# Two layers of long convolution and MLP, forward and backward: moving the next chunk's gates on VectorE and six PSUM copies between VectorE and ScalarE

## The chip, the cores and the metric

The kernel runs on one core of a Trainium2 chip. Its engines are TensorE (PE; PEld is its weight load), VectorE (DVE), ScalarE (ACT), GpSimd (POOL) and SyncE (SP), and 16 DMA engines. The metric is the device time of one execution in microseconds, the median of several runs. Before the change it is 688.22 us (three runs, 687.91 to 688.73).

## The reference

The forward pass has two layers, each a gated long convolution (`A`) and an MLP (`B`), and the same weights serve both. The kernel returns the output and the gradients for eight inputs.

```python
def _A_ref(q, k, v, shift_k, ssm_k, ssm_D):      # S = 2048, D = 448
    kv = (k shifted by 0..3 rows, weighted by shift_k, summed) * v
    y = irfft(rfft(kv padded) * rfft(ssm_k padded))[:S] + kv * ssm_D
    return q * y
def _B_ref(x, w1, w2):                            # F = 1792
    return silu(x @ w1) @ w2
x = A_q
x = x + _A_ref(_layernorm(x), A_k, A_v, A_shift_k, A_ssm_k, A_ssm_D)
x = x + _B_ref(_layernorm(x), B_w1, B_w2)
x = x + _A_ref(_layernorm(x), A_k, A_v, A_shift_k, A_ssm_k, A_ssm_D)
x = x + _B_ref(_layernorm(x), B_w1, B_w2)
# outputs: x, and the gradients of A_q, A_k, A_v, A_shift_k, A_ssm_k, A_ssm_D, w1, w2 for grad_out
```

`k` and `v` do not change between the layers, so the convolution's result `y` is computed once. What a layer's `A` does to `x` is then a normalisation, a multiplication by `y` and an addition: the gate.

## The kernel before

The kernel has three parts. A prefix computes the convolution (up to about 84 us in the profile) and leaves its result in `Ysb`. `Main.run` then goes over the 2048 rows in four chunks of 512 (four tiles of 128 rows), from about 84 to 500 us. A suffix does the weight gradients and the gradients of the convolution.

For each chunk `Main` runs layer 1 (L = 0) and layer 2 (L = 1) forward and then both backward, and it weaves the backward of chunk c with the forward of chunk c + 1. The steps are Python generators, and each step emits one piece:

- `H`: the first product (w1) in 14 blocks of 128 columns, taken in pairs `fp` = 0 to 6. ScalarE writes Silu of a pair to `aT` (L833, or L816 in chunk 0) and a raw copy to `Dall` (L116). `slope` later turns `Dall` into the derivative of Silu in place (L843, six ScalarE instructions and a table load). In chunk 0 `Hh` does the same in half chunks, and VectorE takes some of the raw copies (L117).
- `O`: the second product (w2), one tile of 128 rows at a time, in two halves of seven matmuls (L850). VectorE adds the result to `X` (L855, "the output sum"). The last one traced is kept as `last_o`.
- `G`: the output gradient times w2 transposed, in pairs again (L681 full matmuls, L685 those with 64 rows of contraction). The copy out of PSUM goes to VectorE for the pairs named in `dv`, else to ScalarE. In layer 2 a later multiplication by the slopes stands at L1013. "Block" below means such a pair.
- `N`: the product with w1 transposed (L889) and the backward of the normalisations (`_ln_bwd`, L1063 to L1068, L905 to L917).
- `T` and `transp_half`: TensorE turns rows (L658, L669), and a copy brings them from PSUM to `nT`.
- `fwd0(c)`: layer 1's first half for a chunk. `_ln_parts` takes the statistics of a tile set (L309 to L313), raises the variance to the power -1/2 on POOL (L314) and normalises (L317). `gate` multiplies by `Y` and adds to `X` (L727, L728, two tiles at a time). Then a second `_ln_parts` normalises the new `X` to `n01`. Those rows are what `T` turns for the next `H`.
- `x_load(c)`: two SP DMAs (L739) that bring the chunk's rows of `A_q` to `xq`, a piece behind w1 and w2 in their tiles. They wait until the gates before have read it.

PSUM is shared by tags: `mm` (two buffers of two banks: `H`, `G`), `po` (two of one bank: `O`, `N`), `tr` (two: turned rows, and block 3 of `G`). In `G` the blocks are taken in groups of 2, 3 and 2. The first block of a group is followed at once by the 64-row matmuls of the others, so the banks of the whole group must be free there.

TensorE's instructions keep the order in which the program emits them. On the other engines and their DMA queues a planner orders the instructions: it simulates the kernel, and among those that its simulation takes to be ready it picks the earliest emitted, with two kinds of help. `tc.high_priority()` moves instructions ahead. `tc.issue_after(ins)` puts whatever the block emits on the engine of `ins` behind `ins` in that engine's queue. An engine then works through its queue strictly in order.

The loop over c in `run` begins with the slopes of layer 2, then `fwd0(c + 1)` queued behind `last_b` (the end of the first tile of `N` of layer 1; at c = 0 behind `last_dv`, a copy of `Hh`). Then it weaves `O` of layer 2 (the letter O), `G` of layer 2 (G), the remaining steps of `fwd0` (L, the generator `self.norm`) and `T`. At c = 0 two tiles of `O` and all of `G` have been emitted before the loop, so there is a short weave:

```python
if c == 0:
    weave("OOTOO", O=o, T=self.T(self.n0[1][1], nT, GBLK, engs=(nc.vector, nc.vector)))
```

Each tile of `O` takes two letters. At c = 0 the last output sum emitted before the weave is that of tile 1.

Of the kernel before, what the change touches and what calls it, by code (L numbers as in the profile page):

```python
# [212 lines left out]
def _hd(k, shape, name):  # L213
    return k.hd.tile(shape, BF16, name=name, tag="hd", bufs=3)
# [81 lines left out]
def _ln(k, pool, c, src, si, n_g, groups=((0, 4),), pin=False):  # L296
    for last in _ln_parts(k, pool, c, src, si, n_g, groups, pin):
        pass
    return last
# [39 lines left out]
def _ln_store(k, c, si, n_g):  # L339
    k.nc.gpsimd.dma_start(out=_pm(k.N_d[si][:])[:, 4 * c:4 * c + 4, :], in_=n_g[:])  # L340
# [272 lines left out]
GBLK = [(0, 128), (128, 256), (256, 384), (320, 448)]  # L613


class Main:
# [98 lines left out]
    def parts(fp):  # L715
        return [(0, 2)] if fp != 3 else [(0, 1), (1, 2)]

    def a_fwd(self, c, si, src, n_g, groups):
        _ln(self.k, self.ch, c, src, si, n_g, groups)
        self.gate(c, src, n_g)  # L720

    def gate(self, c, src, n_g, pairs=((0, 2), (2, 4)), pin=lambda i: i):
        nc, X = self.nc, self.X
        for lo, hi in pairs:
# [16 lines left out]
    def fwd0(self, c):  # L741
        k, nc = self.k, self.nc
        n01 = self.t([P, 4, D], "n01", bufs=2)
        if c == 0:
            xc, n00 = k.x0c0, k.na0
            self.first_norm(xc, n00, n01)
        else:
            n00 = _hd(k, [P, 4, D], "n00")
            xc = lambda tl: k.xq[tl.start // 2] if isinstance(tl, slice) else k.xq[tl // 2][:, tl % 2, :]
            self.a_fwd(c, 0, xc, n00, ((0, 4),))  # L750
            self.n0[c] = (n00, n01)
            norm = _ln_parts(k, self.ch, c, self.xs(c), 1, n01, ((0, 4),))
            next(norm)
            self.norm = self.fwd0_end(c, norm, n01)
            return
        _ln_store(k, c, 1, n01)
        self.n0[c] = (n00, n01)
# [8 lines left out]
            next(step)  # L766
        next(steps[1], None)

    def fwd0_end(self, c, norm, n01):
        with self.tc.issue_after(self.last_o.ins):  # L770
            next(norm, None)
        _ln_store(self.k, c, 1, n01)
        yield

# [154 lines left out]
    def run(self, ys):  # L929
        k, nc, tc = self.k, self.nc, self.tc  # L930
        self.n0, self.gyt = {}, {}
        jobs = k.jobs = Jobs(k, self)
        jg = jobs.gen()

        def weave(pattern, **gens):
            for ch in pattern:
                next(gens[ch], None)
            for g in gens.values():
                if g is not jg:
                    for _ in g:  # L940
                        pass

        gT, gh2 = self.nT(), []
        g = self.G(gT, gh2, groups=(1,) * 7)
        tg = self.T(k.gb0, gT, GBLK, engs=(nc.vector, nc.vector))
        nT = self.nT()
        go = lambda *gens: [next(x, None) for x in gens]
        go(tg, tg, ys, ys)
        with tc.high_priority():
            self.fwd0(0)  # L950
        go(ys, ys, ys, ys, ys, ys, g)
        with tc.high_priority():
            self.transp_half(self.n0[0][1], nT, GBLK, 0, nc.vector)
        go(g)
        self.Dall = k.mdp.tile([P, 2, 2, NF // 2, 512], BF16, name="Dall", tag="DA")
        self.w1T = k.wtp.tile([P, NF, D], BF16, name="w1T", tag="WT")
        with tc.issue_after(nc.sync.dma_start_transpose(out=self.w1T[:], in_=k.B_w1).ins):
            self.x_load(1)
        aT, dT1 = self.halves("aT", "T", 5), self.dT(0, 0)
        hs = [self.Hh(0, 0, nT, aT, dT1, 0, (1, 3), (1,)), self.Hh(0, 0, nT, aT, dT1, 1)]  # L960
        os_ = [self.O(0, 0, aT, (0, 1)), self.O(0, 0, aT, (2, 3))]
        go(hs[0], hs[0])
        with tc.high_priority():
            self.transp_half(self.n0[0][1], nT, GBLK, 1)
        go(hs[0], hs[0])
        go(*(hs[1], os_[0]) * 4)
        self.slope(dT1)
        with tc.high_priority():
            self.fwd1(0, ((0, 2),))
        with tc.issue_after(self.last_n.ins):  # L970
            go(*(os_[1],) * 4)
        go(g, g)
        with tc.high_priority():
            self.fwd1(0, ((2, 4),))
        nT = self.nT()
        aT, dT2 = self.halves("aT", "T", 5), self.dT(0, 1)
        hs = [self.Hh(0, 1, nT, aT, dT2, 0, (1, 3), (1,)), self.Hh(0, 1, nT, aT, dT2, 1)]
        r = [aT, dT2]
        with tc.issue_after(self.transp_half(self.n1[1], nT, GBLK, 0).ins):
            nc.scalar.activation(k.warm[:], k.mhalf[:], ACT.Silu)  # L980
        go(g, hs[0], hs[0], hs[0])
        self.transp_half(self.n1[1], nT, GBLK, 1)
        go(hs[0], g)
        o = self.O(0, 1, aT)
        go(*(hs[1], o) * 4, g)
        for c in range(4):

            aT2, dT2 = r
            self.slope(dT2)
            if c < 3:  # L990
                with tc.issue_after((self.last_b if c else self.last_dv).ins):
                    self.fwd0(c + 1)
                if c == 0:
                    next(self.norm)
            if c < 2:
                self.x_load(c + 2)
            nT = self.nT() if c < 3 else None
            if c > 0:
                o = self.O(c, 1, aT2)
            if c == 0:  # L1000
                weave("OOTOO", O=o, T=self.T(self.n0[1][1], nT, GBLK, engs=(nc.vector, nc.vector)))
            else:
                gh2 = []
                g = self.G(gT, gh2, dv=(1, 4))
                if c < 3:
                    weave("OOLOOGOGOGOGGOGTG", O=o, G=g, L=self.norm, T=self.T(self.n0[c + 1][1], nT, GBLK))
                else:
                    self.put()
                    jobs.start()
                    weave("GOOOOOOOOGGGGGG", O=o, G=g)  # L1010
            for hh in range(2):
                for lo, hi in ((0, 4), (4, 7)):
                    nc.vector.tensor_tensor(out=gh2[hh][:, lo:hi, :], in0=dT2[hh][:, lo:hi, :], in1=gh2[hh][:, lo:hi, :], op=ALU.mult)  # L1013
                self.store(("g", 1), gh2[hh], c, hh)
            if c == 3:
                self.put()
            n = self.N(c, 1, gh2, lambda tl: self.X[:, 4 * c + tl, :], self.n1[1], self.n1[0])
            G2 = self.X[:, 4 * c:4 * c + 4, :]
            gT = self.nT()
            gh1, dT0 = [], dT1  # L1020
            tg = self.T(G2, gT, GBLK, "tr" if c < 3 else "mm")
            if c < 3:
                r = []
                weave("NHNHNHNHNHNHNHN", N=n, H=self.H(c + 1, 0, nT, r))
                gT2 = self.nT()
                with tc.issue_after(self.last_xl.ins):
                    _turn_grad(k, c + 1, gT2)
                aT, dT1 = r
                weave("OOOOOOTOO", O=self.O(c + 1, 0, aT), T=tg)
                self.fwd1(c + 1)  # L1030
                weave("GGGGGGG", G=self.G(gT, gh1, dT0))
                self.slope(dT1)
                gT = gT2
            else:
                weave("NNJNJNJNJNJNJNJ", N=n, J=jg)
                weave("J" * 14 + "TJJJ", T=tg, J=jg)
                weave("GGJGJGJGJGJGJ", G=self.G(gT, gh1, dT0, (1, 3, 5), (2, 2, 2, 1)), J=jg)
            for hh in range(2):
                self.store(("g", 0), gh1[hh], c, hh)
            if c == 3:  # L1040
                self.put()
            n = self.N(c, 0, gh1, lambda tl: self.X[:, 4 * c + tl, :], self.n0[c][1], self.n0[c][0])
            if c < 3:
                r = []
                nT = self.nT()
                weave("NNTNNHHNHNHNHNHH", N=n, T=self.T(self.n1[1], nT, GBLK), H=self.H(c + 1, 1, nT, r))
            else:
                k.m1h = []
                for i in range(2):
                    m = _hd(k, [P, 8, 2, P], "M1h")  # L1050
                    nc.gpsimd.dma_start(out=m[:].rearrange("p a c k -> p (a c k)"), in_=k.m1_h.ap()[:, 2048 * i:2048 * (i + 1)])
                    k.m1h.append(m)
                k.A1g = k.mdp.tile([P, NB, 2, 16, 2], BF16, name="A1g", tag="DA")
                k.pt = dict(s1=dict(tag="mm", bufs=2))
                k.bal.reset()
                k.bal.add("dve", 30.0)
                weave("SNJSNJSNJSNJSNJSNJSNJSNJSJSJSJSJ", N=n, J=jg, S=_s1_gy(k, range(12)))
# [415 lines left out]
```

## Time and profile before

| | |
|---|---|
| median of the runs | 688.22 us (687.91 to 688.73) |
| profiled execution | 687.9 us, span 686.1 us |
| granted TensorE clock, mean | 0.999 |
| busy: TensorE, VectorE, ScalarE, POOL | 665.3, 482.2, 429.7, 104.6 us |
| TensorE's idle gaps over 0.1 us | 14.0 us together; longest 1.55, 1.55, 0.90, 0.90, 0.83 |
| loop pass c = 1, from one 1.55 gap to the next | 91.98 us |
| VectorE copy of a block, f32 PSUM 128x1024 (ghT, L117) | 1.22 us, x6 |
| ScalarE copy of a block, the same (ghT, L116) | 1.01 us, x40 |
| copy of turned rows, bf16 PSUM 128x1024 (nT): VectorE, ScalarE | 0.68 us, 1.01 us |
| slopes, 128x1024 and 128x1536 (L843), table load | 1.05, 1.47, 1.28 us |

A line of a timeline gives the start in us from the span's start, the length in us, the engine, the line of the kernel, the operation, what it writes and reads with shapes, and how many instructions are merged; in brackets stands the idle time of the engine just before, and what ended it. A line of a table of waits gives who waited for whom, the total in us, how often, and the longest. A matmul's length holds its latency; successive 128x448 matmuls start 0.19 us apart, and 128x512 ones 0.215.

### The profile page before, as it was taken

The page shows a single profiled execution, that of the slowest core. Times are in us where ns is not written, and L with a number is a line of the kernel's source. Part 1 is how long each engine was busy: PE and PEld are TensorE (multiplying, and loading weights), DVE is VectorE, ACT ScalarE, POOL GpSimd, SP SyncE. Part 2 cuts the span into 40 slices and gives each one's busy share as a digit, 9 for nine tenths or more (in the row PEclk, how much of TensorE's full clock was granted, in tenths as well). Part 3 has the DMA queues.
Part 4 walks back from the last instruction along what each step waited for, and adds up shares of the span by engine and source line. Part 5 has one row for each costly group of instructions (what it writes and reads, how often), then busy time and mean ns, then how long its engine had stood idle before and what let it go on. Part 6 is the DMA issues. An engine that isn't in the chain of part 4 may idle for free.

```text
span 686.1 us, 14467 instructions
## 1 busy us (share of the span) xinstructions
PE 665.3 (97%) x5844; PEld 362.3 (53%) x5879; DVE 482.2 (70%) x1133; ACT 429.7 (63%) x528; POOL 104.6 (15%) x177
## 2 busy tenths in 40 slices
PE   8989999999999899999899999999999999999997
PEld 6876755554444344444444444544555555555666
DVE  5779954677879858898588874843937554528992
ACT  5988987888758668678477685123634543653431
POOL 1047320110010100101001000010111211102311
PEclk9999999999999999999999999999999999999999
DMA  8999989499788767598776799859599988956981
GB/s 316 248 278 316 342 191 227 112 228 258 191 241 228 219 163 193 123 250 231 182 162 193 218 241 375 241 173 205 200 238 354 324 274 323 351 173 223 324 308 42
DMA packets 203956, 162.60 MB, mean 237 GB/s; under 512 B 153505, under 2 KB 184244, under 8 KB 203122
## 3 DMA queue, kind: packets, MB, share of 16 engines
q1 hardware_dynamic: 190806, 113.35, 61.7%
q0 software_dynamic: 11088, 39.84, 17.1%
q10 hardware_dynamic: 1996, 8.49, 3.8%
q8 instruction: 46, 0.75, 0.4%
q14 instruction: 20, 0.16, 0.1%
HBM read 66.05 MB, written 54.60 MB: 176 GB/s over the span
## 4 chain that ended last, share of the span: by engine, by line
PE 77%; DVE 11%; ACT 5%; DMA 3%; issue 2%; POOL 1%; DVEq 0%; POOLq 0%
PE ps_d L1115 25%; PE ps_n L889 11%; PE ps_o L850 9%; PE ps_g L681 9%; PE ps_h L681 7%; PE ps_v L272 2%; PE ps_g L685 2%; PE ps_h L685 2%; DMA spec_K<-KAB 2%; DVE ln_st L309 1%; ACT KAB L116 1%; DVE lb_v L1063 1%; DMA KAB<-KAB 1%; PE ps_gK L1398 1%; PE ps_y L604 1%
## 5 line engine op out<-in xcount | busy, mean ns | idle before, releaser
L1115 PEld LDWEIGHTS <-dstat 128*128 128x128 bf16 x928 | 87.1, 98 | 75.7 <-issue 4.0
L889 PE MATMUL ps_n<-w1T,ghT 128*128 128x448 bf16 x448 | 94.5, 353 | 0.0
L850 PE MATMUL ps_o<-w2sb,aT 128*128 128x448 bf16 x448 | 89.2, 353 | 1.8 <-DVE X L855 1.8
L116 ACT CAST ghT<-ps_g 128x1024 bf16<-128x1024 f32 (+1 forms) x54 | 48.3, 899 | 60.9 <-PE ps_g L685 46.8
L681 PE MATMUL ps_h<-nT,w1sb 128*128 128x512 bf16 (+1 forms) x410 | 83.0, 336 | 2.1 <-DVE Dall L117 0.8
L681 PE MATMUL ps_g<-nT,w2T 128*128 128x512 bf16 x317 | 77.9, 379 | 1.6 <-ACT Dall L116 0.4
L889 PEld LDWEIGHTS <-ghT 128*128 128x128 bf16 x448 | 42.4, 98 | 45.3 <-issue 4.7
L850 PEld LDWEIGHTS <-aT 128*128 128x128 bf16 x448 | 43.2, 98 | 41.8 <-issue 3.5
L681 PEld LDWEIGHTS <-w1sb 128*128 128x128 bf16 x420 | 39.1, 98 | 37.1 <-issue 8.2
L1063 DVE SCALAR_TENSOR_TENSOR lb_v<-lb_u,n 128x448 bf16<-128x448 bf16 x60 | 37.2, 621 | 27.6 <-ACT lb_u L905 27.2
L833 ACT ACTIVATE aT<-ps_h 128x1024 bf16<-128x1024 f32 (+1 forms) x48 | 44.2, 922 | 19.7 <-PE ps_h L681 11.5
L116 ACT CAST Dall<-ps_h 128x1024 bf16<-128x1024 f32 (+2 forms) x60 | 54.8, 913 | 0.0
L843 ACT ACTIVATE Dall<-Dall 128x1024 bf16<-128x1024 bf16 (+1 forms) x48 | 53.3, 1186 | 0.1
L681 PEld LDWEIGHTS <-w2T 128*128 128x128 bf16 x336 | 31.3, 98 | 40.9 <-issue 5.9
L314 POOL TENSOR_TENSOR rstd<-ln_ve,mhalf 128x2 f32<-128x2 f32 (+1 forms) x24 | 19.6, 818 | 183.7 <-DVE ln_ve L313 183.7
L1115 PE MATMUL ps_d<-X,dstat 128*128 128x448 bf16 x224 | 47.6, 353 | 0.0
L1115 PE MATMUL ps_d<-go,dstat 128*128 128x448 bf16 x224 | 47.2, 353 | 0.0
L1115 PE MATMUL ps_d<-n3m,dstat 128*128 128x448 bf16 (+1 forms) x240 | 47.0, 340 | 0.0
L1115 PE MATMUL ps_d<-n1m,dstat 128*128 128x448 bf16 (+1 forms) x240 | 46.5, 340 | 0.0
L116 ACT CAST A1g<-ps_v 128x1024 bf16<-128x1024 f32 x14 | 14.9, 1064 | 36.5 <-PE ps_v L272 36.5
L855 DVE TENSOR_TENSOR X<-X,ps_o 128x448 bf16<-128x448 bf16 x32 | 19.5, 611 | 18.4 <-PE ps_o L850 18.2
L905 ACT ACTIVATE lb_u<-ps_n,rstd 128x448 bf16<-128x448 f32 x32 | 20.5, 639 | 16.8 <-PE ps_n L889 13.0
(210 smaller groups left out, 1111.9 us busy)
## 6 DMA issues: line engine op xcount, KB each, us to landing
dstat<-a_d SPq DMA_DIRECT2D x28, 512.0 KB, 5.0
dstat<-g_d SPq DMA_DIRECT2D x28, 512.0 KB, 5.4
a_d<-turned SPq DMA_DIRECT2D x16, 512.0 KB, 3.0
g_d<-turned SPq DMA_DIRECT2D x16, 512.0 KB, 3.0
a_d<-turned SPq DMA_DIRECT2D x16, 384.0 KB, 2.7
g_d<-turned SPq DMA_DIRECT2D x16, 384.0 KB, 2.8
spec_K<-KAB POOLq DMA_DIRECT2D x7, 512.0 KB, 6.3
KAB<-KAB POOLq DMA_DIRECT2D x28, 128.0 KB, 5.1
```

The costliest lines, as they stand in the source:

```text
L116: return nc.scalar.copy(out, in_)
L314: nc.gpsimd.tensor_tensor(out=r[:, lo:hi], in0=ve[:, lo:hi], in1=k.mhalf[:, lo:hi], op=ALU.pow)
L681: self.nc.tensor.matmul(ps, lhsT=w[:, b, ft * P:(ft + 1) * P], rhs=x[:, b], start=(start and b == 0), stop=(stop and b == bs[2]))
L685: self.nc.tensor.matmul(ps, lhsT=w[sl, b, ft * P:(ft + 1) * P], rhs=x[sl, b], start=start, stop=stop)
L833: self.last_silu = nc.scalar.activation(aT[hh][:, o:o + hi - lo, :], ps(lo, hi), ACT.Silu)
L843: self.nc.scalar.activation(dT[hh][:, o:o + n, :], dT[hh][:, o:o + n, :], ACT.Derivative_silu)
L850: nc.tensor.matmul(po[:, :D], lhsT=aT[ft // 7][:, ft % 7, tl * P:(tl + 1) * P], rhs=self.w2sb[:, ft, :], start=(ft == 0), stop=(ft == NF - 1))
L855: self.last_o = nc.vector.tensor_tensor(out=X[:, t, :], in0=X[:, t, :], in1=po[:, :D], op=ALU.add)
L889: nc.tensor.matmul(pns[tl][:, :D], lhsT=gh[h][:, ft % 7, tl * P:(tl + 1) * P], rhs=self.w1T[:, ft, :], start=(ft == 0), stop=(ft == NF - 1))
L905: nc.scalar.activation(u0[:], pn[:, :D], ACT.Identity, scale=k.rstd[2 * L + 1][:, t:t + 1], accum_out=cp[:, tl, 0:1])
L1063: nc.vector.scalar_tensor_tensor(out=v[:], in0=u0, scalar=-1.0 / D, in1=n_t, op0=ALU.mult, op1=ALU.mult, accum_out=cp[:, 1:2])
L1115: self.nc.tensor.matmul(ps[:, cols], lhsT=st[:, t, :], rhs=mov[:, t, cols], start=(first and t == 0), stop=(last and t == NT - 1))
```

## The change

Four edits. At c = 1 and 2 the gates and the second statistics of the next chunk are no longer traced in `fwd0`. They are the first step of the generator `fwd0_end`, queued behind `last_o`, and the weave takes that step after the first tile of `O` and the normalisation after the second. At c = 0 both steps are taken before the weave. The load of the chunk after (`x_load`) moves into that generator, behind the gates. In layer 2, `G` has all its copies on ScalarE at c = 1 and 2 (`dv` is empty; at c = 3 it stays `(1, 4)`, and at c = 0 all were on ScalarE already). In chunk 0 the copies of the second half's turned rows go to VectorE in both layers. `a_fwd`, which only `fwd0` called, is gone.

```diff
-    def a_fwd(self, c, si, src, n_g, groups):
-        _ln(self.k, self.ch, c, src, si, n_g, groups)
-        self.gate(c, src, n_g)
...
     def fwd0(self, c):
...
-            self.a_fwd(c, 0, xc, n00, ((0, 4),))
+            _ln(k, self.ch, c, xc, 0, n00)
             self.n0[c] = (n00, n01)
-            norm = _ln_parts(k, self.ch, c, self.xs(c), 1, n01, ((0, 4),))
-            next(norm)
-            self.norm = self.fwd0_end(c, norm, n01)
+            self.norm = self.fwd0_end(c, xc, n00, n01)
             return
...
-    def fwd0_end(self, c, norm, n01):
+    def fwd0_end(self, c, xc, n00, n01):
+        norm = _ln_parts(self.k, self.ch, c, self.xs(c), 1, n01, ((0, 4),))
         with self.tc.issue_after(self.last_o.ins):
-            next(norm, None)
+            self.gate(c, xc, n00)
+            next(norm)
+        if c < 3:
+            self.x_load(c + 1)
+        yield
+        with self.tc.issue_after(self.last_o.ins):
+            next(norm)
         _ln_store(self.k, c, 1, n01)
         yield
...
-            self.transp_half(self.n0[0][1], nT, GBLK, 1)
+            self.transp_half(self.n0[0][1], nT, GBLK, 1, nc.vector)
...
-        self.transp_half(self.n1[1], nT, GBLK, 1)
+        self.transp_half(self.n1[1], nT, GBLK, 1, nc.vector)
...
                 if c == 0:
                     next(self.norm)
-            if c < 2:
-                self.x_load(c + 2)
+                    next(self.norm)
...
-                g = self.G(gT, gh2, dv=(1, 4))
+                g = self.G(gT, gh2, dv=(1, 4) if c == 3 else ())
                 if c < 3:
-                    weave("OOLOOGOGOGOGGOGTG", O=o, G=g, L=self.norm, T=self.T(self.n0[c + 1][1], nT, GBLK))
+                    weave("OOLOOLGOGOGOGGOGTG", O=o, G=g, L=self.norm, T=self.T(self.n0[c + 1][1], nT, GBLK))
```

## Prediction

> **What bounds the kernel now.** I read the page's busy times first, then TensorE's table of waits, then the timelines of the stretches where its longest waits lie.
>
> ```profile
> PE 665.3 (97%) x5844; PEld 362.3 (53%) x5879; DVE 482.2 (70%) x1133; ACT 429.7 (63%) x528; POOL 104.6 (15%) x177
> PEclk9999999999999999999999999999999999999999
> ```
>
> TensorE is the bound: its queue is written by hand, it is busy for 97% of the 686.1 us, and its clock is full in every slice. A change can only win where TensorE waits and lose where it makes a new wait. The table of its waits (total, times, longest) says how little there is to win:
>
> ```profile
> PE ps_g L685 <- DVE ghT L117: 3.1, 2, 1.6
> PE ps_o L850 <- DVE X L855: 1.8, 2, 0.9
> ...
> PE ps_h L681 <- DVE Dall L117: 0.8, 1, 0.8
> PE ps_h L681 <- ACT Dall L116: 0.6, 1, 0.6
> ```
>
> These four rows are the ones that the diff touches: 6.3 us. The first two come twice, in the passes c = 1 and c = 2; the others once, in chunk 0. TensorE's timeline of pass c = 1 shows where they stand:
>
> ```profile
> 229.06 1.48 PE L850 MATMUL ps_o<-w2sb,aT 128*128 128x448 bf16 x7 [0.90 <-DVE X L855]
> ...
> 233.00 1.46 PE L681 MATMUL ps_g<-nT,w2T 128*128 128x512 bf16 x6
> 234.39 0.60 PE L685 MATMUL ps_g<-nT,w2T 64*128 64x512 bf16 x4
> 236.55 0.39 PE L685 MATMUL ps_g<-nT,w2T 64*128 64x512 bf16 x2 [1.55 <-DVE ghT L117]
> ...
> 243.96 0.63 PE L658 MATMUL ps_t<-ident,n 64*128 64x64 bf16 x32
> ```
>
> At 228.16 the output sum's third tile needs the PSUM bank that VectorE's first output sum empties; at 235.00 the gradient's block 4 needs the bank that VectorE's copy of block 1 empties. At 243.96 the next chunk's normalised rows are turned. VectorE and ScalarE in the same stretch:
>
> ```profile
> 228.39 0.62 DVE L855 TENSOR_TENSOR X<-X,ps_o 128x448 bf16<-128x448 bf16 x1
> ...
> 234.05 1.31 DVE L317 TENSOR_SCALAR n<-X,ln_mv,rstd 128x448 bf16<-128x448 bf16 x4 [1.81 <-POOL rstd L314]
> 235.28 1.22 DVE L117 CAST ghT<-ps_g 128x1024 bf16<-128x1024 f32 x1
> ```
>
> ```profile
> 224.53 6.64 ACT L843 ACTIVATE Dall<-Dall 128x1024 bf16<-128x1024 bf16 x6
> 231.07 0.99 ACT L116 CAST ghT<-ps_g 128x1024 bf16<-128x1024 f32 x1
> 234.82 1.01 ACT L116 CAST ghT<-ps_g 128x1024 bf16<-128x1024 f32 x1 [2.76 <-PE ps_g L685]
> ```
>
> The first output sum's matmuls end at about 223.7, but VectorE reaches it only at 228.39, behind the backward tail of layer 1, four gate instructions and two statistics. The copy of block 1 is ready to start at 231.7 and stands until 235.28 behind a normalisation that waits for POOL. ScalarE meanwhile has gaps of 2.76, 3.22 and 3.66 us.
>
> **The change, part by part.**
>
> *Gates behind the first output sum (c = 1, 2).* Four gate instructions (L727, L728, 0.53 apart, 2.1 us) and two statistics with one aggregate (1.2 us) go from before the sum to after it. Before the sum only the tail of layer 1's backward is left on VectorE. From 221.25 it has 16 instructions; at the spacing that the trace shows for such chains when nothing else fills them (0.43 between dependent short ones, 0.55 to 0.72 after the long ones, as from 251.56 on) it ends by about 227.1. The sum then ends by 227.7 at the latest, and TensorE asks at 228.16: the 0.90 goes, both times. What is late next: TensorE comes to block 2 at 233.00 - 0.90 = 232.10, and needs block 0's bank, which ScalarE empties by 232.07 behind its slopes: 0.02 is lost, no more. Gain 0.88 each; ends 0 (if the planner puts the sum no earlier) and 0.90.
> Behind the sum now queue the gates, four statistics, the second sum and the normalisation. VectorE's work to that point is the same in another order, so the normalised rows come at about 235.5, as now (235.36); TensorE asks for them at 243.96 - 2.45 = 241.5. On POOL the power stands behind the issue of two stores (0.58 and 0.54), as now. Six us cover all that: cost nothing, and one for one beyond them.
>
> *Gradient blocks 1 and 4 on ScalarE (c = 1, 2).* Two copies of 1.22 leave VectorE, two of 1.01 come to ScalarE, into its gaps. Block 1 is copied from 232.0 to 233.1; TensorE, shifted, asks for that bank at about 234.3. The 1.55 goes, both times. Block 4 would be copied by 239.4 in the shifted time, asked for at 241.4. Gain 1.55 each; ends 1.0 (if ScalarE were half a us late on both) and 1.55.
>
> *Second halves' turned rows on VectorE (chunk 0).* In layer 2, ScalarE's copy (1.03 from 131.69) stands before a Silu whose matmuls end at about 131.95. Without it the Silu (0.84) ends at 132.8, VectorE's copy of the same bank (0.96) at 133.8 in place of 134.43: of 0.83 some 0.2 is left, gain 0.63. VectorE takes 0.68 for the moved copy (row "nT<-ps_t", x14, 684 ns) and is free from 130.93 to 133.47. In layer 1 the wait of 0.61 ends with a ScalarE pair that started at 100.06, when its matmuls had ended at about 99.97: gain 0.09. Ends 0.5 and 0.9 together; taken 0.72.
>
> *The loads of A_q* are queued on SP after the gates, now at about 228 and, for chunk 1's pass, 148. Behind them on SP stand the transposes of aT and their stores; the buffers they free are wanted over 8 us later, so nothing.
>
> *What the same edit does at c = 0.* Here both steps of the chain are taken before the weave, and `last_o` is the sum of the second tile, not the first. VectorE and TensorE there:
>
> ```profile
> 139.49 1.15 DVE L727 TENSOR_TENSOR a_t<-n,Ysb 128x896 bf16<-128x896 bf16 x2
> ...
> 144.74 0.17 DVE L313 TENSOR_SCALAR ln_ve<-ln_mv 128x4 f32<-128x4 f32 x1
> 146.28 0.62 DVE L855 TENSOR_TENSOR X<-X,ps_o 128x448 bf16<-128x448 bf16 x1 [1.37 <-PE ps_o L850]
> 146.82 1.35 DVE L317 TENSOR_SCALAR n<-X,ln_mv,rstd 128x448 bf16<-128x448 bf16 x4
> ```
>
> ```profile
> 150.55 0.64 PE L658 MATMUL ps_t<-ident,n 64*128 64x64 bf16 x32
> ```
>
> Now the gates and statistics of chunk 1 run in idle time of VectorE before that sum, and only the normalisation is behind it; it is done 2.4 us before TensorE turns the rows. After the change all of it is behind the sum. From the sum's start: 0.54 to the next instruction, gates 2.14 (139.49 to 141.63), statistics 2.75 (the same eight and one took 134.35 to 137.10), the power on POOL 1.15 (137.10 to 138.25; the store issue there, 147.20 to 147.80, is past by then), normalisation 1.32: 7.90. 146.28 + 7.90 = 154.18 against 150.55: TensorE stands 3.6 us, 3.5 if the first transposes overlap. The planner may fill the wait for POOL with the third tile's sum (0.54) and the first gradient product (1.14), which are ready then: 1.68 in a hole of 1.15, 0.5 more. I take 4.0, between 3.5 and 4.2. TensorE shows no wait from 150 to 228, so nothing gives it back. The products that follow on VectorE would then be ready 0.1 to 0.2 before TensorE needs them; if that margin goes, tenths more.
>
> *Sum:* -0.72 - 2 x 0.88 - 2 x 1.55 + 4.0 = -1.58 in the profiled execution, 687.9 (span 686.1 and 1.8 around it), which is 0.3 under the median of 688.22. Against the median: 686.6. Ends of the terms: -0.9 - 1.8 - 3.1 + 3.5 = -2.3, and -0.5 - 0 - 2.0 + 4.2 = +1.7; the likeliest case's own range is 685.9 to 687.9, as only one term is likely to fail.
>
> **Rivals.**
>
> *No stall at c = 0.* If chunk 1's chain kept to the idle time before the sum, the gain would be 5.6: 682.6. Against it: the normalisation sits straight behind that sum now (146.82), so the edge is obeyed. 0.08.
>
> *The waits of c = 1, 2 only move.* The planner orders VectorE by its own clock, not the chip's; if the first sum stays as late as it is (0.88) and ScalarE's slopes run 0.3 later, 2 x 1.2 of the gain goes: 689.0. For it: ScalarE empties block 0 only 0.03 before TensorE asks. Against: nothing else is left to put before the sum. 0.14.
>
> *The clock drops in the new gap.* The longest gap that TensorE has today is 1.55, and its clock stays full; the start shows the other pace: ten 128x512 matmuls take 4.34 us, 434 ns each, where six take 1.29 later, 215 each. A gap of 4.0 is over twice what the trace shows to be harmless. If it is enough, about 4.1 us (first matmul at 1.19 to the full clock at 5.3) run at half pace: 2.05 lost, 688.7; twice that if it falls twice, 690.7. 0.10.
> [...]
>
> *Slower: the gradient products slip in front of chunk 1's normalisation.* Place: VectorE's queue at c = 0. If the planner has all four L1013 products ready before POOL's power is back, the normalisation waits for the last slope (ScalarE, 155.31) and the last product (0.95 and its wait), to start at 156.4 in place of 152.9: a stall of 7.1, the sum +1.5, 689.8. It is slower from a stall of 5.6 on, that is from three products on. For it: the products are next in rank. Against: three of the four need slopes that end at 152.05 or later, when the power is nearly back. 0.13.
>
> **How the numbers follow.** Forecast 0.50, rivals 0.08, 0.14, 0.10, 0.13, and 0.05 for what I do not see. A measurement of this kernel can tell about 0.2%, 1.4 us, from no change. The forecast of -1.6 is only just outside: two thirds of it count as faster, a third as same. Faster: 0.34 of the forecast, 0.08, 0.02 of the moved waits, 0.01 unseen: 0.45. Same: 0.16 of the forecast, 0.12 of the moved waits, 0.05 of the clock: 0.33. Slower: 0.13, 0.05 of the clock, 0.04 unseen: 0.22. The range 684.6 to 689.8 leaves out the first rival, the clock's dearer end and the unseen.
>
> **What would show it.** In TensorE's waits after: no `ps_g L685 <- DVE ghT`; no or a shorter `ps_o L850 <- DVE X`; `ps_h L681 <- DVE Dall` at 0.2; and a new row of about 4 us, ps_t L658 waiting for VectorE's n L317, once. The pass from c = 1 to c = 2 (236.87 to 328.85 now) should be 2.4 us shorter. I am wrong if the ps_t wait is missing or well over 4.2, if ps_g waits for ScalarE's ghT by more than 0.1, or if the clock leaves 1.00 after 150.

## The result, and the profile after

The changed kernel takes 690.22 us (median of 8 runs, 689.55 to 691.43) against 688.12 in the same comparison (687.83 to 688.75): ratio 1.0027, 95% interval 1.0018 to 1.0036. It is slower by 2.1 us where 1.6 less was forecast, and 690.22 lies above the forecast range of 684.6 to 689.8. The profiled execution took 689.88 us with a span of 687.9. In the changed kernel, and in the trial kernels made from it, the lines of the program have shifted: L851 is L850 of before, L856 is L855, L890 is L889, and the gates are L723 and L724.

TensorE's table of waits after the change (total us, times, longest):

```profile
PE ps_t L658 <- DVE n L317: 4.8, 1, 4.8
...
PE ps_h L681 <- ACT Dall L116: 0.6, 1, 0.6
...
PE ps_h L681 <- DVE Dall L117: 0.3, 1, 0.3
```

Three of the four rows of before are gone or shrunk, as forecast: ps_g no longer waits for VectorE's ghT, ps_o no longer for X, and ps_h for VectorE's Dall only 0.3 in place of 0.8. The fourth, ps_h for ScalarE's Dall, is still 0.6. In place of the others stands one new wait, of 4.8 us. It is the one that the prediction charged against the change, at c = 0. TensorE's timeline there:

```profile
147.50 2.82 PE L851 MATMUL ps_o<-w2sb,aT 128*128 128x448 bf16 x14
155.10 1.79 PE L658 MATMUL ps_t<-ident,n 64*128 64x64 bf16 x32 [4.78 <-DVE n L317]
156.83 4.19 PE L851 MATMUL ps_o<-w2sb,aT 128*128 128x448 bf16 x14
160.85 1.49 PE L890 MATMUL ps_n<-w1T,ghT 128*128 128x448 bf16 x7
```

Two things are to be seen. The rows are turned 4.78 us after TensorE is free for it. And what follows is slow: 14 matmuls of the output sum took 2.82 ahead of the wait, from 147.50, and 14 of the same shape take 4.19 behind it, and the 32 little transposes 1.79 where they took 0.64. The windows of the same execution say why (columns: stretch, its length, busy time of TensorE, weight load, VectorE, ScalarE and POOL, granted clock, DMA):

```profile
149.40:152.80 3.40, 0.93 (x5) 0.29 (x3) 3.40 (x11) 3.40 (x5) 0.00 (x0) 1.00 1.16 264
152.80:156.20 3.40, 0.88 (x14) 0.50 (x16) 2.48 (x7) 3.38 (x3) 1.66 (x1) 0.50 1.15 347
156.20:159.60 3.40, 3.40 (x34) 1.73 (x29) 2.96 (x4) 0.13 (x1) 0.60 (x1) 0.50 1.16 294
```

The granted clock was 0.50 from 152.8 to 159.6. It fell in the middle of the wait and came back 4.5 us after TensorE had resumed.

VectorE shows why the wait is longer than worked out:

```profile
150.92 0.16 DVE L310 BATCH_NORM_AGGREGATE ln_mv<-ln_st 128x2 f32<-128x6 f32 x1
151.00 0.58 DVE L856 TENSOR_TENSOR X<-X,ps_o 128x448 bf16<-128x448 bf16 x1
151.51 0.17 DVE L310 BATCH_NORM_AGGREGATE ln_mv<-ln_st 128x2 f32<-128x6 f32 x1
151.60 1.19 DVE L1013 TENSOR_TENSOR ghT<-Dall,ghT 128x2048 bf16<-128x2048 bf16 x1
152.71 0.16 DVE L313 TENSOR_SCALAR ln_ve<-ln_mv 128x4 f32<-128x4 f32 x1
152.78 0.94 DVE L1013 TENSOR_TENSOR ghT<-Dall,ghT 128x1536 bf16<-128x1536 bf16 x1
154.65 1.31 DVE L317 TENSOR_SCALAR n<-X,ln_mv,rstd 128x448 bf16<-128x448 bf16 x4 [0.92 <-POOL rstd L314]
```

The third output sum and the first gradient product do not fill the hole in which POOL raises the power. They stand before the last small instruction (L313) on which POOL waits, so all of their 1.6 us is added. The second product then runs while POOL works, and POOL's instruction takes 1.66 in place of 1.01:

```profile
152.96 1.66 POOL L314 TENSOR_TENSOR rstd<-ln_ve,mhalf 128x4 f32<-128x4 f32 x1 [5.47 <-DVE ln_ve L313]
```

In the passes c = 1 and 2 it went as worked out. Pass c = 1, TensorE:

```profile
235.21 1.48 PE L851 MATMUL ps_o<-w2sb,aT 128*128 128x448 bf16 x7
...
239.15 1.46 PE L681 MATMUL ps_g<-nT,w2T 128*128 128x512 bf16 x6
240.54 0.82 PE L685 MATMUL ps_g<-nT,w2T 64*128 64x512 bf16 x6
241.30 1.50 PE L851 MATMUL ps_o<-w2sb,aT 128*128 128x448 bf16 x7
```

No bracket is left: the third tile of the output sum and the 64-row matmuls of block 4 start without a wait.

TensorE's order of instructions is the same in both kernels, so each instruction can be set against its twin. How far the changed kernel is behind, start by start: +0.27 from the prefix on (which the change does not touch), -0.29 from 134 us on, +7.01 after the weave of c = 0, then +6.15 and +4.43 at the two spots of pass c = 1, +3.56 and +1.85 at those of c = 2, and +1.86 at the end. So chunk 0 gains 0.56, the weave of c = 0 costs 7.30 (the expectations below say 7.25), and the passes c = 1 and 2 gain 2.58 and 2.57.

### The profile page after: what moved, and what is told of

It reads as the page before. It is cut to its first block, busy times and chain, and to the rows that moved or that the text cites. A ratio compares the mean times of both kernels' runs of the same rounds, so it can differ in the third digit from the quotient of the medians.

```text
span 687.9 us, 14465 instructions
## 1 busy us (share of the span) xinstructions
PE 667.5 (97%) x5844; PEld 363.2 (53%) x5879; DVE 480.0 (70%) x1131; ACT 431.9 (63%) x530; POOL 105.2 (15%) x177
## 4 chain that ended last, share of the span: by engine, by line
PE 87%; DVE 4%; ACT 3%; issue 3%; DMA 1%; POOL 1%; POOLq 0%; DVEq 0%
PE ps_d L1115 25%; PE ps_n L890 13%; PE ps_o L851 12%; PE ps_h L681 10%; PE ps_g L681 10%; PE ps_h L685 2%; PE ps_v L272 2%; PE ps_g L685 2%; ACT KAB L116 1%; PE ps_gK L1398 1%; PE ps_y L604 1%; PE ps_gkv L1369 1%; PE ps_t L658 1%; PE ps_s L225 1%; DVE KAB L117 1%
## 5 line engine op out<-in xcount | busy, mean ns | idle before, releaser
L890 PE MATMUL ps_n<-w1T,ghT 128*128 128x448 bf16 x448 | 94.4, 353 | 0.0
L851 PE MATMUL ps_o<-w2sb,aT 128*128 128x448 bf16 x448 | 90.6, 356 | 0.1
L116 ACT CAST ghT<-ps_g 128x1024 bf16<-128x1024 f32 (+1 forms) x58 | 52.2, 906 | 52.4 <-PE ps_g L685 39.3
L890 PEld LDWEIGHTS <-ghT 128*128 128x128 bf16 x448 | 42.5, 98 | 45.1 <-issue 5.1
L851 PEld LDWEIGHTS <-aT 128*128 128x128 bf16 x448 | 43.6, 99 | 41.5 <-issue 3.7
L856 DVE TENSOR_TENSOR X<-X,ps_o 128x448 bf16<-128x448 bf16 x32 | 19.4, 610 | 27.4 <-PE ps_o L851 27.4
```

The source lines that it names most:

```text
L116: return nc.scalar.copy(out, in_)
L851: nc.tensor.matmul(po[:, :D], lhsT=aT[ft // 7][:, ft % 7, tl * P:(tl + 1) * P], rhs=self.w2sb[:, ft, :], start=(ft == 0), stop=(ft == NF - 1))
L856: self.last_o = nc.vector.tensor_tensor(out=X[:, t, :], in0=X[:, t, :], in1=po[:, :D], op=ALU.add)
L890: nc.tensor.matmul(pns[tl][:, :D], lhsT=gh[h][:, ft % 7, tl * P:(tl + 1) * P], rhs=self.w1T[:, ft, :], start=(ft == 0), stop=(ft == NF - 1))
```

## Experiments

Theory A: all of the loss stands at c = 0 and has two parts, a wait for chunk 1's normalised rows and a halved clock behind it; the rest of the change gains what was forecast. Theory B: the loss is spread over the planner's new orders. Theory C: the slow matmuls behind the wait are late for their inputs, and the clock is no cause.

**The gates of c = 0 put back** (`c0_early`):

```diff
-        with self.tc.issue_after(self.last_o.ins):
+        with self.tc.issue_after(self.last_o.ins) if c > 1 else nullcontext():
             self.gate(c, xc, n00)
             next(norm)
```

`fwd0_end` is called with the number of the next chunk, so its c = 1 belongs to the pass c = 0 of the loop.

> The change with one part undone: at c = 0 chunk 1's gates and statistics are not queued behind the output sum (c = 1, 2 as in the change). Theory A, the whole loss stands at c = 0 (TensorE 7.25 us later there: a wait of 4.8 and 2.5 at half clock) and the rest of the change gains 5.7: no wait of ps_t for n, clock 1.00 throughout, 690.2 - 7.25 = 683.0, 0.9925 of before. Theory B, the loss is spread over the planner's new order elsewhere: 686 to 690, and waits of 0.5 us or more in other places.

Measured: 682.93 us (682.47 to 683.51), ratio to before 0.9921 (0.9908 to 0.9933). That is theory A's 683.0. No wait of ps_t is in its table, and the weave of c = 0 runs as it did before the change, at full clock (granted 1.00 from 146 to 160 us):

```profile
150.22 0.64 PE L658 MATMUL ps_t<-ident,n 64*128 64x64 bf16 x32
150.79 2.82 PE L851 MATMUL ps_o<-w2sb,aT 128*128 128x448 bf16 x14
```

Theory B falls. This version is faster than both kernels; against the one before it gains 5.4 us.

**That part alone** (`only_c0`): the change with its other parts undone. Gates and second statistics stay behind `last_o` at c = 0; at c = 1 and 2 they are traced ahead of the weave, behind `last_b`, as before, and the copies of layer 2's gradient and of the turned rows are where they were. Only the load of A_q keeps its new place, as it does in `c0_early`. From the edit against the change:

```diff
-        with self.tc.issue_after(self.last_o.ins):
+        with self.tc.issue_after(self.last_o.ins) if c == 1 else self.tc.issue_after(self.last_b.ins):
             self.gate(c, xc, n00)
             next(norm)
...
-                g = self.G(gT, gh2, dv=(1, 4) if c == 3 else ())
+                g = self.G(gT, gh2, dv=(1, 4))
```

> The kernel before with one part of the change alone: chunk 1's gates and statistics behind the output sum at c = 0; at c = 1, 2 they are traced before the weave as before, the copies stay where they were. Theory A: 688.1 + 7.25 = 695.4, the four waits of before still there. Theory B: 689 to 692.

Measured: 695.95 us, ratio 1.0109 (1.0095 to 1.0123). The new wait is 4.8 again, and the four of before are all there:

```profile
PE ps_t L658 <- DVE n L317: 4.8, 1, 4.8
PE ps_g L685 <- DVE ghT L117: 3.1, 2, 1.6
PE ps_o L851 <- DVE X L856: 1.8, 2, 0.9
```

The loss needs nothing of the copies, the turned rows or the order at c = 1 and 2.

**TensorE kept busy in the wait** (`fill20`):

```diff
+    def W(self, x):
+        ps = self.k.psum.tile([P, 2, 512], FP32, name="ps_fill", tag="mm", bufs=2)
+        for i in range(20):
+            self.nc.tensor.matmul(ps[:, 0, :], lhsT=self.w2sb[:, 0, 0:P], rhs=x[0][:, 0, :], start=True, stop=True)
+        yield
...
-                weave("OOTOO", O=o, T=...)
+                weave("OOWTOO", W=self.W(aT2), O=o, T=...)
```

> The change, with 20 matmuls of 128x512 whose result nobody reads put on TensorE right before it turns chunk 1's rows (20 x 0.215 = 4.3 us, inside the 4.8 that it waits). Theory A, the matmuls behind the gap are slow because the clock was halved by the idle time: the clock stays 1.00, the next 14 matmuls start 0.19 apart, the rows are turned at the same time, 690.2 - 2.5 = 687.7. Theory C, they are slow because their inputs come late: 690.2, and the 14 matmuls still 0.29 to 0.38 apart.

Measured: 688.75 us, ratio to before 1.0005 (0.9996 to 1.0013).

```profile
150.90 4.48 PE L929 MATMUL ps_fill<-aT,w2sb 128*128 128x512 bf16 x20
155.84 1.47 PE L658 MATMUL ps_t<-ident,n 64*128 64x64 bf16 x32 [0.46 <-DVE n L317]
157.24 2.82 PE L851 MATMUL ps_o<-w2sb,aT 128*128 128x448 bf16 x14
```

```profile
150.00:160.00 10.00, 9.23 (x73) 4.50 (x72) 8.97 (x20) 7.04 (x7) 2.25 (x2) 1.00 1.09 305
```

The 14 matmuls take 2.82 again, and the granted clock is 1.00 throughout; its mean over the whole kernel is 0.999 or 1.000 in all twelve runs. Twenty matmuls of useless work make the kernel faster, because the clock stays up: theory C falls. The gain is less than the 2.5 expected: against their befores the two kernels stand at +2.1 and +0.4, 1.7 apart. The expectation had put down all of the slow transposes to the clock, but at full clock they still take 1.47, since each tile's rows arrive 0.31 after the last (four normalisations take 1.31, one alone 0.39). By starts against the kernel before, the weave of c = 0 costs 5.60 here and 7.30 with the clock halved, so 1.7 was the clock and 5.6 the wait (0.32 of the 1.7 in the transposes, 1.37 in the 14 matmuls).

**Nothing in front of the normalisation** (`no_slip`): at c = 0 the weave and the four products are queued behind chunk 1's normalisation.

```diff
+                with tc.issue_after(self.last_norm.ins):
                     weave("OOTOO", ...)
...
+                    with tc.issue_after(self.last_norm.ins) if c == 0 else nullcontext():
                         nc.vector.tensor_tensor(out=gh2[hh][:, lo:hi, :], ...)
```

> The change, with the third and fourth output sums and layer 2's four gradient products of chunk 0 queued behind chunk 1's normalisation on VectorE, so that nothing slips into its chain. If the chain then takes what the prediction worked out (7.9 us from the sum's start), the wait is 3.6 in place of 4.8 and the power on POOL 1.03 in place of 1.65. With the clock still halved, less long: about 688.5; if 3.6 is too short to halve it: 690.2 - 1.2 - 2.5 = 686.5. If the power still takes 1.65, VectorE's products were not what slowed it.

Measured: 688.44 us (685.55 to 690.73), ratio 0.9989 (0.9972 to 1.0006). The chain from the second output sum's start to the last normalised row takes 7.89 (146.60 to 154.49), for 7.90 in the prediction. POOL takes 1.02 as soon as no product runs beside it:

```profile
152.12 1.02 POOL L314 TENSOR_TENSOR rstd<-ln_ve,mhalf 128x4 f32<-128x4 f32 x1 [4.02 <-DVE ln_ve L313]
```

The gap is 2.69 before the first transposes, where 3.6 was expected. The 3.6 counted to the last row; TensorE starts with the first, and as the rows come 0.31 apart the transposes take 1.47 in place of 0.64. Together that is a delay of 3.5.

```profile
153.63 1.47 PE L658 MATMUL ps_t<-ident,n 64*128 64x64 bf16 x32 [2.69 <-DVE n L317]
155.03 4.51 PE L851 MATMUL ps_o<-w2sb,aT 128*128 128x448 bf16 x14
```

The spread is the finding. The mean granted clock sorts the twelve runs into three groups of four: 1.000 with 685.6 to 686.8 us, 0.997 to 0.998 with 688.2 to 688.9, and 0.994 to 0.995 with 689.2 to 690.7. The profiled run (0.998) has one halved stretch, of 3.4 us. By that, an estimate from the mean clocks, the groups have no such stretch, one, and two; the traces of the others are not kept. The first group is 2.4 us below the second and 3.7 below the third. That is more than the clock can make: at half pace a stretch of 3.4 us loses 1.7 at most, and in the trace the 14 matmuls take 4.51 for 2.82, 1.69 more. What the rest is stays open. The kept traces do show other differences between executions, of under 1 us: TensorE waits 0.8 us in `fill20` and 0.9 in `only_order` for a DMA into `dstat`, and the changed kernel's table of waits has no such row.

**The rows turned one tile later** (`turn_late`):

```diff
-                    weave("OOTOO", O=o, T=...)
+                    weave("OOOOT", O=o, T=...)
```

> The change, with chunk 1's rows turned behind the fourth output sum's matmuls in place of the third's (weave OOOOT). TensorE then asks 2.65 us later. If the wait shrinks by just that: 690.2 - 2.65 = 687.6. If the gap, now about 2, also leaves the clock at 1.00, it is 2 less, 685.6; but the turned rows' copies are then wanted at once, and up to 1.9 may come back as a wait of ps_h for nT.

Measured: 687.69 us (686.06 to 689.63), ratio 0.9990 (0.9979 to 1.0001). The wait falls to 2.12 and no wait for nT comes back; but the clock halves even then, for one stretch in this execution:

```profile
153.00:156.40 3.40, 1.09 (x8) 0.34 (x6) 2.48 (x7) 3.38 (x4) 1.65 (x1) 1.00 1.03 352
156.40:159.80 3.40, 3.31 (x35) 1.76 (x36) 3.40 (x6) 0.64 (x1) 1.14 (x2) 0.51 1.17 297
```

So the first of the two expectations, 687.6, is met by the median, and the second's condition, a gap harmless to the clock, was not met in this execution. Two of the eleven runs kept a mean clock of 0.999 and took 686.1 and 686.6.

**Each gaining part alone.** The copies of layer 2's gradient on ScalarE (`only_copies`):

```diff
-                g = self.G(gT, gh2, dv=(1, 4))
+                g = self.G(gT, gh2, dv=(1, 4) if c == 3 else ())
```

> The kernel before with one part of the change alone: at c = 1, 2 all copies of layer 2's gradient blocks on ScalarE. If the parts add up: the two waits of 1.55 for ghT go, the two of 0.90 for the output sum stay: 688.4 - 3.1 = 685.3. If ScalarE becomes the late one behind its slopes, new waits of ps_g for ScalarE's ghT and less than half of it: over 686.9.

Measured: 685.59 us, ratio 0.9962 (0.9950 to 0.9974), with the waits of 0.90 left as they were. The edit gains 1.73 by the starts in each of the passes c = 1 and c = 2.

The order alone, at c = 1 and 2 (`only_order`: `c0_early` with the copies of layer 2's gradient and of the turned rows as before, so the moved load stays in):

> The kernel before with one part alone: at c = 1, 2 gates and second statistics behind the first output sum (c = 0 as before, copies as before). If the parts add up: the two waits of 0.90 go, 688.4 - 1.8 = 686.6. If VectorE's copy of block 1 stays where it is, behind the normalisation, TensorE only waits there for as much longer (2.4 in place of 1.55, twice), and it is 688.4, no gain.

Measured: 691.84 us (691.09 to 694.53), ratio 1.0061 (1.0046 to 1.0076). This misses both expectations, in the direction of the second.

```profile
PE ps_g L685 <- DVE ghT L117: 6.0, 2, 3.0
```

```profile
227.83 0.61 DVE L856 TENSOR_TENSOR X<-X,ps_o 128x448 bf16<-128x448 bf16 x1
...
234.93 1.31 DVE L317 TENSOR_SCALAR n<-X,ln_mv,rstd 128x448 bf16<-128x448 bf16 x4 [1.15 <-POOL rstd L314]
236.16 1.22 DVE L117 CAST ghT<-ps_g 128x1024 bf16<-128x1024 f32 x1
```

The wait of 0.90 is gone. The copy of block 1, still on VectorE, stands behind the normalisation 0.6 later than before (0.9 by the two timelines, of which this execution loses 0.3 in the prefix), while TensorE comes 0.9 earlier. The wait there is 2.99 in place of 1.55, twice. After the first of them the clock halves, after the second it does not:

```profile
234.80:238.20 3.40, 0.77 (x5) 0.36 (x5) 3.17 (x6) 0.48 (x1) 0.69 (x2) 1.00 0.38 135
238.20:241.70 3.50, 3.50 (x11) 1.34 (x10) 1.04 (x2) 0.27 (x1) 0.00 (x0) 0.51 0.79 207
...
327.00:330.40 3.40, 1.68 (x10) 0.50 (x8) 2.22 (x11) 1.01 (x1) 1.02 (x1) 1.00 0.40 124
330.40:333.80 3.40, 2.13 (x12) 1.03 (x12) 2.97 (x4) 0.00 (x0) 0.60 (x1) 1.00 0.37 146
```

Moving the gates gains its 0.9 a pass only with the copies moved too; alone it costs.

The turned rows (`only_turned`):

> The kernel before with one part alone: in chunk 0 the second halves' turned rows copied by VectorE. Wait of ps_h for Dall 0.83 to 0.27, the other of 0.61 as it is: 688.4 - 0.56 = 687.8. If TensorE waits elsewhere for it: 688.4.

Measured: 688.34 us, ratio 0.9998 (0.9990 to 1.0007). The trace shows the shift of 0.56 at 134 us; the runs cannot tell it from nothing, and 687.8 lies inside their interval too.

## Why the prediction was wrong

Point by point, by its own steps.

- *Gates behind the first output sum, c = 1, 2.* Right in effect: 0.88 forecast for each pass, 0.86 measured (+7.01 to +6.15, +4.43 to +3.56). It was nearer than worked out. VectorE's tail of layer 1 takes 6.27 (228.27 to 234.54) where 5.85 was allowed, and the sum ends 0.06 before TensorE starts the third tile, where 0.46 was allowed: that hardly any of the gain was lost is in part luck. The rows were normalised at 242.96 and asked for at 248.38, 5.4 us of cover for the 6 worked out. What the prediction did not say is that this gain hangs on the copies (`only_order`).

```profile
234.54 0.61 DVE L856 TENSOR_TENSOR X<-X,ps_o 128x448 bf16<-128x448 bf16 x1
...
241.64 1.31 DVE L317 TENSOR_SCALAR n<-X,ln_mv,rstd 128x448 bf16<-128x448 bf16 x4 [1.15 <-DMA out_dram<-X]
...
248.38 0.63 PE L658 MATMUL ps_t<-ident,n 64*128 64x64 bf16 x32
```

- *Blocks 1 and 4 on ScalarE.* Right: 1.55 forecast, 1.72 measured in each pass.
- *Turned rows on VectorE.* 0.72 forecast, 0.56 measured; the wait of 0.61 did not move (0.6 after), the other left 0.27.
- *Loads of A_q on SP.* Right: no wait of it is in any table.
- *The step that failed is the cost at c = 0.* It was taken at 4.0, between 3.5 and 4.2, and measured 7.30. The place, the cause and the chain itself were right: with the chain undisturbed it takes 7.89 (`no_slip`), 7.90 worked out, and the delay is 3.5. Two things in it were wrong. First, what slips in: the prediction let 1.68 of VectorE's work fill POOL's hole and charged 0.5. It stood in front of the instruction that starts POOL (1.6), and POOL was slowed by the next product (1.66 for 1.02). That cost 2.1, and the wait came to 5.6. Second, the clock, which the sum put at nothing: 1.7 here. The prediction named it as a rival with a chance of 0.10 and a price of 2.05.

Two of the signs that the prediction gave for being wrong came true: the ps_t wait well over 4.2, and a clock that left 1.00 after 150.

Sum with the measured terms, in the profiled spans: -0.56 - 2.58 - 2.57 + 5.6 + 1.7 = +1.6, and +0.27 of the prefix makes the 1.86 by which the changed kernel is behind at the end. With neither the slip nor the clock, in the four runs of `no_slip` at full clock, the kernel takes 685.6 to 686.8, about the 686.6 of the forecast.

The rival of the dropping clock decided it together with the longer wait. Its argument was sound (the gap was far over what the trace showed to be harmless), and its chance was too low for that. No run shows the 0.10; it was the author's estimate. The runs showed the clock fall inside the gap of 4.78 and after gaps of 2.99, 2.69 and 2.12 us, the last two with scattered transposes behind them. In the 3.4 us ahead of a fall TensorE was busy for 0.77 (`only_order`), 0.93 (the change), 1.09 (`turn_late`) and 1.36 us (`no_slip`). With 1.68 of 3.40 busy, around the second gap of 2.99 in `only_order`, it stayed up, and with 1.85, around the 1.55 gap of the kernel before:

```profile
234.00:237.40 3.40, 1.85 (x12) 0.61 (x10) 3.25 (x6) 1.01 (x1) 0.61 (x2) 1.00 0.45 158
```

Two gaps of one length can thus end differently. In the clock records of the two kernels' traces the times between changes are whole numbers of stretches of 3.413 us: 679.25 us before the change (199 of them, from 5.29 to 684.54), and 146.77, 6.83 and 529.07 after it (43, 2 and 155, from 6.03 to 152.81, 159.63 and 688.70). The first rise to full clock thus came at 5.29 us in one and at 6.03 in the other. If the stretches run on from that rise in every execution, which is the author's estimate from these records, their cuts fall at another place of the gap each time. The first gap of `only_order` leaves its stretch (234.8 to 238.2) 0.77 us of work. The second is cut so that its stretch (327.0 to 330.4) keeps 1.68.

The rival "products in front of the normalisation" described the right mechanism too, with two products and not four. Its price was worked out without the clock, so both dear cases were priced as if they excluded each other. By the mean granted clock of the runs, the clock fell in all twelve with a wait of 4.8 (the change and `only_c0`), and in 17 of the 23 with 2.7 or 2.1 (`no_slip`, `turn_late`).

## What to carry to other kernels

An edit to a loop's body is to be costed in every pass, the odd first one above all: here the same queue edge gains 0.86 where the chain behind it has 5 us of cover and costs 7.30 where it has none. A new wait of TensorE is not priced by its length alone: here the clock stayed full through waits of 1.55 us and fell after one of 2.12, and of two of 2.99 it fell after the first only. Ask what share of the 3.4 us around it is still busy (1.36 us was followed by half clock here, 1.68 by full), and add the halved clock with a chance (1.7 us by the traces here). And when a chain on VectorE has a hole that POOL fills, see whether other work can be queued ahead of the instruction that opens the hole, and pin the chain if it can.

## What the runs showed of the hardware

The clock halved after a gap as short as 2.12 us (`turn_late`). It stayed halved for 6.83 us after the change (0.50 from 152.81 to 159.63), and for about 3.4 in the profiled executions of `no_slip` (0.50 from 155.3 to 158.7), `turn_late` (0.51 from 156.4 to 159.8) and `only_order` (0.51 from 238.2 to 241.7). Stretches of 3.4 us with 0.77 (`only_order`), 0.93 (the change), 1.09 (`turn_late`) and 1.36 us (40%, `no_slip`) of TensorE's busy time were followed by half clock, and stretches with 1.68 (49%, `only_order`) and 1.85 (54%, before) by full clock. Whether a gap of this size halves the clock varies from run to run of one program: four of twelve runs of `no_slip` have a mean clock of 1.000, the other eight 0.994 to 0.998. Work that nobody needs, put into the gap, prevented it (`fill20`: 0.999 or 1.000 in all twelve runs).

POOL's power on 128x4 values took 1.01 before the change and 1.66 after it, when VectorE multiplied two bf16 tiles beside it. In `no_slip`, where the products are queued behind the normalisation, it is 1.02 again; in `turn_late`, with a product beside it, 1.65. After the change the product ran from 152.78 to 153.72, and POOL, which began at 152.96, ended at 154.62, 0.9 after the product. Why POOL takes longer then was not shown.
